# Weight conversion in the lead-in of a linear-attention and ELU-MLP kernel: first splits and lowerings earlier, most merges on GpSimd

## The chip, the cores and the metric

The kernel runs on one core of one Trainium2 chip. The metric is the device time in microseconds (us) of one execution; a time is the median of several runs. Engines are called by the names of the profile: PE (TensorE, the matrix engine; PEld is its weight load), DVE (VectorE), ACT (ScalarE), POOL (GpSimd) and SP (SyncE, which here only starts DMA transfers). Each engine works through its own queue in the order in which the program wrote the instructions; between engines, semaphores order the work.

## What is computed

The reference, cut to what matters:

```python
# attention: q, k, v, f_logit are (4, 8, 768, 48), float32
f = 1.0 / (1.0 + np.exp(-f_logit))
for t in range(S):
    state = f[:, :, t, :, None] * state + einsum('bhd,bhe->bhde', k[:, :, t], v[:, :, t])
    y[:, :, t] = einsum('bhd,bhde->bhe', q[:, :, t], state)
# mlp: x = y as (3072, 384); w_in (384, 2048), w_out (2048, 384), both float64
h = x @ w_in
g = np.where(h > 0.0, h, np.exp(np.minimum(h, 0.0)) - 1.0)
out = (g @ w_out).astype(np.float32)
```

The weights arrive in 64-bit floating point. The kernel turns them into 32-bit floating point itself, on the chip, while the first tokens are already being worked on. That conversion is what the change is about.

## The kernel before

Tokens are worked on in 12 units of 256. The attention of a unit writes `xt`; the MLP of the unit then multiplies it with `w_in` (an "up" product into the PSUM tile `psH`), applies the ELU and multiplies with `w_out` (a "down" product into `psM`). The weights are cut into 16 **items** of 128 x 768 numbers: eight blocks of `w_in` and eight of `w_out`, sorted by when the MLP first needs them. Items 0, 1, 2, 4, 6, 8 are the blocks 0 to 5 of `w_in`; items 3, 5, 7, 9, 10, 11 are the blocks 0 to 5 of `w_out`; items 12 to 15 are the last two of each.

Every item passes through four stages: `fetch` (DMA of the raw 64-bit words into one of AHEAD = 7 slots of `area`), `split` (two DVE instructions on the high halves), `lower` (one ACT instruction, which brings the top bits of the low halves into place) and `merge` (one 32-bit integer addition, after which the slot is free and the fetch seven items later is started).

```python
def split(n):
    raw = raws[n]
    hi = raw.bitcast(I32)[:, 1::2]
    bits = held[n] = sb.tile([128, 2 * DM], I32, tag="bits", name=f"bits{n}")   # two buffers, in turn
    nc.vector.tensor_scalar(out=bits[:], in0=hi, scalar1=3, scalar2=0x3FFFFFF8,          # L559
                            op0=ALU.logical_shift_left, op1=ALU.bitwise_and)
    nc.vector.tensor_scalar(out=hi, in0=hi, scalar1=-(2**30), scalar2=None, op0=ALU.bitwise_and)  # L563

def lower(n):
    nc.scalar.activation(raw.bitcast(U16)[:, 2::4], raw.bitcast(U32)[:, 0::2], AF.Copy, scale=2.0**-29)  # L569

def merge(n):
    ...
    nc.vector.tensor_tensor(out=to.bitcast(I32), in0=bits, in1=hi, op=ALU.add)            # L577
    fetch(n + AHEAD)
```

Other helpers that stand in the same stretch: `fall(u, p)` is a DVE reciprocal (L627), `scale(...)` a GpSimd multiplication of a 128x256 piece of q or k (L617), `move(u, which, queue)` two small DMAs from `f` to `f` (L634), started here from ACT's queue, `transposed` four PE transposes and an ACT copy (L665, L669), `first_outputs` the attention output of unit 0 (L804) with the ACT copies into `xt` (L814, L816), `watch` a tiny DVE check. The end of the lead-in, before the change:

```python
    step(0, NC - 1)
    split(0)
    ...                                   # GpSimd copies; fetches of items 2 to 6
    fall(1, 1)
    first_outputs(0)
    lower(0)
    merge(0)
    first_outputs(1)
    scale(1, ...k and q of pairs 0 to 2, on GpSimd...)
    split(1)
    transposed(1, 0, "a0")
    warm(1)                               # a matmul without use, for the PE clock
    transposed(1, 1, "a1")
    lower(1)
    watch(0)
    scale(1, ("q", 1, nc.gpsimd))
    fall(1, 2)
    scale(1, ("q", 2, nc.gpsimd))
    move(1, 1, nc.scalar)
    watch(1)
    at_step(1, lambda: scale(1, ("q", NKT, nc.gpsimd)))
    attention(1, (), A1)                  # attention of unit 1, its parts at the steps A1
    for n in range(1, NFT):
        t = max(needs[n][0] - 2, 0)       # two steps before the MLP needs item n
        at_step(t, lambda n=n: merge(n))
        if n > 1:
            later.setdefault(max(t - 2, 0), []).append(n)
```

After it comes a loop over steps T; two steps are one pair of an up product P = T // 2 and a down product P - 2:

```python
    for T in range(NU * NFT):
        P = T // 2
        if T % 2 == 0 and P and order[P - 1][0] < DIRECT:
            elu(P - 1)                    # DVE, L932: reads psH of P - 1 and so frees it
        for f in plan.pop(T, ()):         # what at_step put there
            f()
        if T % 2 == 0:
            up(P)                         # 12 matmuls, L923; psH has two buffers; then two ACT passes, L910, L911
        elif P >= LAG:
            down(P - LAG)                 # 8 matmuls, L955
        for n in later.pop(T, ()):
            split(n)
            lower(n)
```

The items 1 to 5 merge at the steps 0, 2, 3, 4, 5; items 6 to 15 at the steps 6, 7, 8, 9, 11, 13, 16, 20, 21 and 25. The attention of unit 1 has its parts `advance` (PE, L724), `step` (five DVE instructions, L682 and L687), `scores` and `mask` (PE L701, DVE L709), `outputs` (PE L739) and `carried` (PE L759) at the steps A1[1] to A1[5].

Of the kernel before, what the change touches and what calls it, by code (L numbers as in the profile page):

```python
# [9 lines left out]
I32 = mybir.dt.int32  # L10
# [3 lines left out]
ALU = mybir.AluOpType  # L14
# [342 lines left out]
def fast(ctx: ExitStack, tc: tile.TileContext, q, k, v, f_logit, w_in, w_out, out, flag, outer):  # L357
# [18 lines left out]
    nc = tc.nc  # L376
# [17 lines left out]
    LAG = 2  # L394
    AHEAD = 7
    WA = 1
    W0 = 3
    HOLD = 2
    A1 = (2, 4, 4, 5, 7, 9)
    D2 = (14, 16, 18, 20)  # L400
    A2 = (22, 24, 24, 26, 27, 28)
    D3 = (-7, -5, -3, -1)
# [67 lines left out]
    for y in first_y:  # L470
# [7 lines left out]
        out=causal[:], in_=causal[:], compare_op=ALU.is_ge, fill=0.0, base=0,  # L478
# [51 lines left out]
    def fetch(n):  # L530
        if n >= NFT:
            return
        j, out_ = parts[n]
        c = slice(j * 256, (j + 1) * 256)
        to = wo[:, 2 * j : 2 * j + 2] if out_ else wi[j][:]
        if wide:
            raws[n] = area[:, n % AHEAD]
            to = raws[n].rearrange("p (k f) -> p k f", k=to.shape[1])
        if out_:
            nc.sync.dma_start(out=to, in_=w_out[c, :].rearrange("(n p) f -> p n f", n=2))  # L540
            return
        nc.sync.dma_start(out=to[MAIN], in_=w_in[0 : NKT * 2 * D, c].rearrange("(k q) f -> q k f", k=NKT))
        rest = w_in[NKT * 2 * D :, c].rearrange("(r d k) f -> r d k f", r=2, d=PAD)
        for r in range(2):
            nc.sync.dma_start(out=to[GAP[r] : GAP[r] + PAD], in_=rest[r])
# [6 lines left out]
    def split(n):  # L552

        if not wide or n >= NFT:
            return
        raw = raws[n]
        hi = raw.bitcast(I32)[:, 1::2]
        bits = held[n] = sb.tile([128, 2 * DM], I32, tag="bits", name=f"bits{n}")
        nc.vector.tensor_scalar(  # L559
            out=bits[:], in0=hi, scalar1=3, scalar2=0x3FFFFFF8,  # L560
            op0=ALU.logical_shift_left, op1=ALU.bitwise_and,
        )
        nc.vector.tensor_scalar(out=hi, in0=hi, scalar1=-(2**30), scalar2=None, op0=ALU.bitwise_and)  # L563

    def lower(n):

        if wide and n < NFT:
# [4 lines that stand above are left out]
        if wide and n < NFT:  # L572
            hi = raws.pop(n).bitcast(I32)[:, 1::2]
            j, out_ = parts[n]
            to = wo[:, 2 * j : 2 * j + 2] if out_ else wi[j][:]
            bits, hi = (x.rearrange("p (k f) -> p k f", k=to.shape[1]) for x in (held.pop(n)[:], hi))
            nc.vector.tensor_tensor(out=to.bitcast(I32), in0=bits, in1=hi, op=ALU.add)  # L577
        fetch(n + AHEAD)


# [32 lines left out]
    def scale(u, *todo):  # L613

        t = qkf[u % NB]
        for n, p, e in todo:
            e.tensor_tensor(out=t[n][:, p], in0=t[n][:, p], in1=t["f"][:, p, "kq".index(n)], op=ALU.mult)  # L617
# [6 lines left out]
    def fall(u, p):  # L624

        f = qkf[u % NB]["f"]
        nc.vector.reciprocal(f[:, p, 1], f[:, p, 0])  # L627

    def move(u, which, queue):

        f = qkf[u % NB]["f"]
        for r in range(2):
            to = PAD + D * r
            queue.dma_start(out=f[to : to + D, NKT, which], in_=f[GAP[r] : GAP[r] + PAD, 0:NKT, which])  # L634
# [38 lines left out]
    def step(u, c):  # L673

        if u % UPB == UPB - 1 and c == NC - 1:
            return
        new = pus[u][c % 2][:, c // 2]
        box = boxes[(u * NC + c) % len(boxes)]
        s = box[:].rearrange("n (p d) -> n p d", d=64)[:, 0:HP, PAD:]
        if u % UPB or c:  # L680
            old = sts[u, c][:].rearrange("n (p d) -> n p d", d=64)[:, 0:HP, PAD:]
            nc.vector.tensor_tensor(out=s, in0=new, in1=old, op=ALU.add)  # L682
        else:
            nc.scalar.copy(s, new)
        if c == NC - 1:
            end = qkf[u % NB]["f"][:, :, 1, U - 1 :].broadcast_to([128, HP, D])
            nc.vector.tensor_tensor(out=s, in0=s, in1=end, op=ALU.mult)  # L687
        sts[(u, c + 1) if c < NC - 1 else (u + 1, 0)] = box
# [18 lines left out]
    def mask(u, pc):  # L707
        for r in range(2):
            nc.vector.tensor_tensor(  # L709
                out=ats[u][:, r].rearrange("k w p i -> k (w p) i"), in0=pc[r][:].rearrange("k w p i -> k (w p) i"),  # L710
                in1=twice[:].unsqueeze(1).broadcast_to([128, NW * HP, C]), op=ALU.mult,
            )
# [62 lines left out]
    def first_outputs(part):  # L775


        q_, at = qkf[0]["q"], ats[0]
        for gap in range(2):
            for w in range(NW):  # L780
                for p in range(NKT):
                    for r in range(2):
                        h = 2 * p + r
                        for b in range(2):
                            c = 2 * w + b
                            if part and c == 0:
                                continue
                            pair = NKT if gap else p
                            if gap:
                                cols = slice((1 - r) * PAD, (3 - r) * PAD)  # L790
                                lhs = (
                                    padded_s[FULL[r], c - 1, p, cols] if part
                                    else padded_v[FULL[b], w, r * NKT + p, cols]
                                )
                            elif part:
                                lhs = sts[0, c][FULL[r], 64 * p + r * PAD : 64 * (p + 1)]
                            else:
                                lhs = vs[0][FULL[b], w, PAD + h * D : PAD + (h + 1) * D] if r else even_v[FULL[b], w, p]
                            rhs = (
                                q_[FULL[r], pair, c * C : (c + 1) * C] if part else at[FULL[b], r, w, pair]  # L800
                            )
                            g = 64 * (r ^ b)
                            to = slice(g + 32 * r, g + 32 * r + 32) if gap else slice(g, g + (D if r else 64))
                            nc.tensor.matmul(  # L804
                                first_y[b][to, w, p], lhsT=lhs, rhs=rhs,
                                start=(part == gap == w == p == 0), stop=(part == 1), skip_group_check=True,
                            )
        if part == 0:
            for b in range(2):
                nc.scalar.copy(between[:, :, 0:NKT], first_y[b][:, :, :, 0])  # L810
            return
        x = xts[0] = sb.tile([128, HP + 1, U], FP32, tag="xt", name="xt0", bufs=3)
        to = x[:, 0:NKT].rearrange("n p (w b i) -> n b w p i", b=2, i=C)
        nc.scalar.copy(to[:, 0], first_y[0][:])  # L814
        for r in range(2):
            nc.scalar.copy(to[FULL[r], 1], first_y[1][FULL[1 - r]])  # L816

    plan, later = {}, {}

    def at_step(step, *todo):  # L820
        plan.setdefault(step, []).extend(todo)
# [218 lines left out]
    for n in range(1, HOLD):  # L1040
        fetch(n)
    warm(W0, "m3")
    for p in range(NKT):
# [7 lines left out]
    scale(0, ("q", 0, nc.gpsimd))  # L1051
    warm(WA, "m3")
    gates(1, bias=0)
# [28 lines left out]
    scores(0, None, (NKT,), pc)  # L1082
    warm(1)
    fall(1, 0)
    for c in range(NC - 1):
        step(0, c)
    mask(0, pc)
    step(0, NC - 1)
    split(0)
    for c in range(NC - 1):  # L1090
        nc.gpsimd.tensor_copy(
            padded_s[:, c, :, PAD : 2 * PAD],
# [4 lines left out]
        nc.gpsimd.memset(area[:, HOLD:].bitcast(I32)[:, :, 0:1], 0)  # L1097
    for n in range(HOLD, AHEAD):
        fetch(n)
    fall(1, 1)  # L1100
    first_outputs(0)
    lower(0)
    merge(0)
    first_outputs(1)
    scale(1, ("k", 0, nc.gpsimd), ("q", 0, nc.gpsimd), ("k", 1, nc.gpsimd), ("k", 2, nc.gpsimd))
    scale(1, ("k", NKT, nc.gpsimd))
    split(1)
    transposed(1, 0, "a0")
    warm(1)
    transposed(1, 1, "a1")  # L1110
    lower(1)
    watch(0)
    scale(1, ("q", 1, nc.gpsimd))
    fall(1, 2)
    scale(1, ("q", 2, nc.gpsimd))
    move(1, 1, nc.scalar)
    watch(1)
    at_step(1, lambda: scale(1, ("q", NKT, nc.gpsimd)))
    attention(1, (), A1)
    for n in range(1, NFT):  # L1120
        t = max(needs[n][0] - 2, 0)
        at_step(t, lambda n=n: merge(n))
        if n > 1:
            later.setdefault(max(t - 2, 0), []).append(n)
    at_step(4, lambda: load(2))
    at_step(12, lambda: gates(2))
    attention(2, D2, A2)
# [6 lines left out]
    for u in range(3, NU):  # L1134
        t = (u - 1) * NFT
# [4 lines left out]
    for n in range(NR):  # L1140
        t = 3 * NFT + (NU - 4) * NFT * n // NR + RR
# [73 lines left out]
```

## Time and profile before

| what | value |
|---|---|
| time | 569.17 us, median of 3 runs (569.11 to 569.18) |
| span of the profiled execution | 567.4 us |
| busy: PE, DVE, ACT, POOL | 550.2, 395.2, 229.3, 266.3 us |
| first up product starts | 29.25 us |
| L559, L563 (a split) on DVE | 0.56 us each in the median, 16 of each |
| L569 (a lowering) on ACT | 1.93 us in the median, 16 times |
| L577 (a merge) on DVE | 0.96 us in the median, 16 times |
| additions and multiplications on POOL | 128x128: 0.455 us (L942), 128x256: 0.72 us undisturbed (L617) |

How to read it: the span is the profiled execution from its first to its last instruction, a little less than the device time. Busy times are sums over the whole span and hide that the first 45 us are quite unlike the rest; so the queries by stretch of time matter more here than the totals. In a group line, the part after the first bar is the busy time in us and the mean in ns, the part after the second bar the engine's idle time before these instructions, with what ended it. In a timeline line, the columns are start, duration, engine, line and operation; square brackets give the idle time before it and what ended that.

### The profile page before, as it was taken

How to read it: one execution, taken by the hardware profiler on the slowest of the kernel's cores; microseconds unless marked ns; L12 is line 12 of the kernel's file. 1: busy time of each engine (PE TensorE's matmuls, PEld its weight loads, DVE VectorE, ACT ScalarE, POOL GpSimd, SP SyncE). 2: the span in 40 equal slices, each digit the busy share in tenths (PEclk: the TensorE clock that was granted, in tenths of full speed). 3: DMA queues.
4: the chain of work that ended last, by engine and by line, in shares of the span. 5: the costliest groups of instructions: out<-in, count | busy, mean ns of one | idle time of the engine just before them, and what ended most of it. 6: DMA issues, size and time to landing. Idle time of an engine off the chain costs nothing.

```text
span 567.4 us, 15202 instructions
## 1 busy us (share of the span) xinstructions
PE 550.2 (97%) x6226; PEld 501.8 (88%) x6226; DVE 395.2 (70%) x765; ACT 229.3 (40%) x417; POOL 266.3 (47%) x530
## 2 busy tenths in 40 slices
PE   6879999999999999999999999999999999999996
PEld 3457777778999999999999999999999999999995
DVE  8798485835976795885785885786786876745543
ACT  3297737334343443434333343343333343333331
POOL 6510027642374474465366357257257348325332
PEclk9998999999999999999999999999999999999999
DMA  8989780060025125215216216216206203201001
GB/s 207 259 215 297 174 223 14 2 161 29 2 50 140 58 60 143 73 45 152 79 36 155 85 37 154 84 38 154 84 20 172 84 9 72 85 2 36 29 2 35
DMA packets 37902, 53.27 MB, mean 94 GB/s; under 512 B 3680, under 2 KB 27648, under 8 KB 37824
## 3 DMA queue, kind: packets, MB, share of 16 engines
q1 hardware_dynamic: 37024, 51.62, 34.6%
q8 instruction: 51, 0.84, 0.6%
q10 hardware_dynamic: 800, 0.59, 0.5%
q14 instruction: 27, 0.22, 0.1%
HBM read 44.04 MB, written 4.72 MB: 86 GB/s over the span
## 4 chain that ended last, share of the span: by engine, by line
PE 92%; DVE 3%; DMA 2%; issue 1%; ACT 1%; POOL 1%; SPq 0%; DVEq 0%; ACTq 0%; POOLq 0%
PE psH L878 35%; PE psM L977 33%; PE psM L955 8%; PE psH L923 6%; PE psS L701 2%; PE psY L739 2%; PE psY L759 2%; PE psU_a L724 2%; PE psT L665 2%; DMA f<-f 1%; DVE f L627 1%; DMA f<-in_f_logit_dram 1%; ACT area L569 1%; DVE bits L559 0%; PE psY L804 0%
## 5 line engine op out<-in xcount | busy, mean ns | idle before, releaser
L878 PE MATMUL psH<-xt,wi 128*128 128x128 f32 (+1 forms) x960 | 177.1, 293 | 0.0
L942 POOL TENSOR_TENSOR sums<-gg 128x128 f32<-128x128 f32 x160 | 69.5, 455 | 210.8 <-DVE gg L932 202.5
L878 PEld LDWEIGHTS psH<-xt,wi 128*128 128x128 f32 x960 | 135.9, 192 | 0.8
L910 ACT ACTIVATE gg<-hh 128x512 f32<-128x512 f32 x80 | 50.5, 631 | 205.9 <-DVE hh L900 140.5
L878 PE MATMUL psH<-xt,area 128*128 128x128 f32 x640 | 110.5, 275 | 0.0
L878 PEld LDWEIGHTS psH<-xt,area 128*128 128x128 f32 x640 | 96.9, 192 | 4.1
L887 DVE TENSOR_TENSOR hh<-psH,u 128x256 f32<-128x256 f32 x80 | 33.8, 423 | 88.7 <-ACT u L885 88.7
L977 PE MATMUL psM<-area,sums 128*128 128x192 f32 x480 | 91.2, 326 | 0.0
L977 PEld LDWEIGHTS psM<-area,sums 128*128 128x128 f32 x480 | 80.1, 190 | 0.2 <-POOL sums L942 0.2
L977 PE MATMUL psM<-wo,gg 128*128 128x192 f32 x320 | 68.1, 335 | 0.0
L617 POOL TENSOR_TENSOR k<-k,f 128x256 f32<-128x256 f32 x48 | 39.4, 822 | 57.1 <-DMA area<-in_moe_w_in_dram 35.0
L627 DVE RECIPROCAL f<-f 128x256 f32<-128x256 f32 x36 | 62.8, 1747 | 1.3
L911 ACT ACTIVATE gg<-gg 128x512 f32<-128x512 f32 x96 | 60.6, 631 | 3.0
L932 DVE SCALAR_TENSOR_TENSOR gg<-gg,hh 128x512 f32<-128x512 f32 x80 | 55.7, 696 | 1.8 <-ACT gg L911 1.8
L977 PEld LDWEIGHTS psM<-wo,gg 128*128 128x128 f32 x320 | 50.2, 190 | 1.9
L900 DVE TENSOR_TENSOR hh<-psH,u43h 128x256 f32<-128x256 f32 (+1 forms) x160 | 49.8, 353 | 2.7
L923 PE MATMUL psH<-xt,wi 128*128 128x256 f32 x192 | 44.5, 381 | 1.4 <-DVE wi L577 1.2
L942 POOL TENSOR_TENSOR sums<-gg,sums 128x128 f32<-128x128 f32 x80 | 42.8, 535 | 6.3
L955 PE MATMUL psM<-wo,gg 128*128 128x384 f32 x128 | 45.4, 498 | 0.0
L885 ACT COPY u<-psH 128x128 f32<-128x128 f32 x80 | 21.0, 263 | 59.3 <-PE psH L878 59.3
L923 PEld LDWEIGHTS psH<-xt,wi 128*128 128x128 f32 x192 | 35.9, 190 | 8.6 <-issue 1.6
L900 DVE TENSOR_TENSOR u43h<-psH,hh 128x256 f32<-128x256 f32 x80 | 33.9, 423 | 13.4 <-PE psH L878 13.0
(97 smaller groups left out, 721.9 us busy)
## 6 DMA issues: line engine op xcount, KB each, us to landing
area<-in_moe_w_out_dram SPq DMA_DIRECT2D x8, 768.0 KB, 8.9
again<-in_moe_w_in_dram SPq DMA_DIRECT2D x16, 384.0 KB, 4.1
again<-in_moe_w_out_dram SPq DMA_DIRECT2D x16, 384.0 KB, 3.5
k<-in_k_dram SPq DMA_DIRECT2D x12, 384.0 KB, 4.8
q<-in_q_dram SPq DMA_DIRECT2D x12, 384.0 KB, 5.5
v<-in_v_dram SPq DMA_DIRECT2D x12, 384.0 KB, 5.9
area<-in_moe_w_in_dram SPq DMA_DIRECT2D x8, 576.0 KB, 7.2
out_dram<-o SPq DMA_DIRECT2D x38, 96.0 KB, 1.7
```

Source lines behind the costliest of these rows:

```text
L617: e.tensor_tensor(out=t[n][:, p], in0=t[n][:, p], in1=t["f"][:, p, "kq".index(n)], op=ALU.mult)
L627: nc.vector.reciprocal(f[:, p, 1], f[:, p, 0])
L878: nc.tensor.matmul(to, lhsT=lhs, rhs=rhs, start=(n == 0), stop=True, skip_group_check=True)
L887: add = lambda to, x, y: nc.vector.tensor_tensor(out=to, in0=x, in1=y, op=ALU.add)
L900: add = lambda to, x, y: nc.vector.tensor_tensor(out=to, in0=x, in1=y, op=ALU.add)
L910: nc.scalar.activation(g[:], h, AF.Relu, scale=-1.0)
L911: nc.scalar.activation(g[:], g[:], AF.Exp, scale=-1.0)
L923: nc.tensor.matmul(ph[:, i], lhsT=wi[j][:, kt, i * 128 : (i + 1) * 128], rhs=xts[m][:, kt, :], start=(kt == 0), stop=(kt == NKT - 1),)
L932: nc.vector.scalar_tensor_tensor(out=g[:], in0=g[:], scalar=-1.0, in1=phs.pop(P), op0=ALU.add, op1=ALU.max)
L942: nc.gpsimd.tensor_tensor(out=s[:, i], in0=x, in1=y, op=op)
L955: nc.tensor.matmul(pm[t][:], lhsT=g[:, i, t * 128 : (t + 1) * 128], rhs=wo[:, 2 * j + i, :], start=(j == 0 and i == 0), stop=(j == NP - 1 ...
L977: nc.tensor.matmul(pm[bank][:, half * DH : (half + 1) * DH], lhsT=x, rhs=y, start=first, stop=(j == NP - 1), skip_group_check=True,)
```

## The change

It reorders the conversion of the first items and moves most merges to another engine:

- `split(0)` and `lower(0)` stand before the mask of unit 0, `split(1)` and `lower(1)` where those of item 0 were, `merge(0)` right after the fetches.
- Both reciprocals that were left, `fall(1, 1)` and `fall(1, 2)`, follow one another, and `move(1, 1)` stands before the transposes.
- The split and lowering of items 2 and 3 come in step 0, ahead of the first up product, instead of after steps 0 and 1.
- Merges of item 2 and later run on GpSimd (M0 = 2); items 0 and 1 stay on DVE.
- The attention parts of unit 1 called `step`, `scores` and `outputs` come at the steps 5, 7, 8 instead of 4, 5, 7.

It is meant to have the weights ready sooner and to take work off the vector engine in the stretch in which that engine is fullest.

```diff
+    M0 = 2
-    A1 = (2, 4, 4, 5, 7, 9)
+    A1 = (2, 4, 5, 7, 8, 9)
@@ merge
-            nc.vector.tensor_tensor(out=to.bitcast(I32), in0=bits, in1=hi, op=ALU.add)
+            e = nc.gpsimd if n >= M0 else nc.vector
+            e.tensor_tensor(out=to.bitcast(I32), in0=bits, in1=hi, op=ALU.add)
@@ lead-in
     fall(1, 0)
+    split(0)
     for c in range(NC - 1):
         step(0, c)
+    lower(0)
     mask(0, pc)
     step(0, NC - 1)
-    split(0)
+    split(1)
 ...
     for n in range(HOLD, AHEAD):
         fetch(n)
+    merge(0)
     fall(1, 1)
+    fall(1, 2)
     first_outputs(0)
-    lower(0)
-    merge(0)
+    lower(1)
     first_outputs(1)
     scale(1, ("k", 0, nc.gpsimd), ("q", 0, nc.gpsimd), ("k", 1, nc.gpsimd), ("k", 2, nc.gpsimd))
     scale(1, ("k", NKT, nc.gpsimd))
-    split(1)
+    move(1, 1, nc.scalar)
     transposed(1, 0, "a0")
     warm(1)
     transposed(1, 1, "a1")
-    lower(1)
     watch(0)
-    scale(1, ("q", 1, nc.gpsimd))
-    fall(1, 2)
-    scale(1, ("q", 2, nc.gpsimd))
-    move(1, 1, nc.scalar)
+    scale(1, ("q", 1, nc.gpsimd), ("q", 2, nc.gpsimd))
     watch(1)
 ...
         if n > 1:
-            later.setdefault(max(t - 2, 0), []).append(n)
+            if t > 3:
+                later.setdefault(t - 2, []).append(n)
+            else:
+                at_step(0, lambda n=n: (split(n), lower(n)))
```

## Prediction

> **What bounds the kernel.** I first asked for the busy times by stretch.
>
> ```profile
> 29.10:45.00 15.90, 11.65 (x168) 9.47 (x166) 14.37 (x25) 13.62 (x13) 2.05 (x2) 0.96 0.87 219
> 45.00:62.00 17.00, 17.00 (x179) 11.95 (x179) 12.56 (x19) 12.15 (x14) 0.00 (x0) 0.94 1.06 284
> 62.00:125.00 63.00, 63.00 (x488) 46.55 (x487) 39.28 (x51) 31.16 (x41) 29.83 (x53) 1.00 0.42 106
> 125.00:280.00 155.00, 155.00 (x1861) 148.28 (x1860) 111.97 (x230) 59.76 (x122) 75.36 (x147) 1.00 0.28 77
> ```
>
> The columns are length, then PE, PEld, DVE, ACT and POOL busy, granted clock, DMA share, GB/s. From 45 us PE has no idle time at all; only the 5.4 us after its last product, at the very end, are without it. So a merge taken off DVE is worth nothing by itself, and the change can only pay before 45 us: by PE's waits there, and by a clock below 1. In that stretch DVE is 14.37/15.90 = 90% and ACT 86% busy, while POOL has 2.05 us of work. Next, the waits of PE and the chain of waits:
>
> ```profile
> PE psS L701 <- issue: 2.6, 1, 2.6
> ...
> PE psH L923 <- DVE wi L577: 1.2, 1, 1.2
> ...
> PE psS L701 <- DVE state L682: 0.2, 1, 0.2
> PE psH L923 <- PE psU_a L724: 0.2, 1, 0.2
> ```
>
> ```profile
> 34.27 1.96 ACT area L569
> ...
> 36.25 0.97 DVE wi L577
> 37.24 0.98 DVE bits L559
> ...
> 38.72 0.96 DVE wo L577
> 39.70 0.57 DVE bits L559
> ...
> 40.78 0.68 DVE gg L932
> ```
>
> In the first the numbers are us in total, times, longest; in the second start, length, engine and tile. The first up product starts at 29.25, the second waits 1.25 us for the merge of item 1 (on DVE from 31.98), and the scores of unit 1 wait 2.6 + 0.2 us: they need the state steps, which stand in DVE's queue behind the splits and merges of items 2 to 5. With the 0.2 us after `advance`, PE's waits after 29.25 sum to **4.25 us**. The last wait also costs clock: by one-us stretches it falls to 0.82 from 43 to 44, is 0.50 from 44 to 47 and 0.97 in the next, together 3.4 us at half speed. There the eight matmuls of the first down product take 3.81 us on the chain, later ones 2.58: **1.2 us** more. The ceiling is 4.25 + 1.2 = 5.5 us, 1.0% of 569.
>
> **What the Trainium skill says.** Three pages bear on it. "GPSIMD Engine Reference", section 4.1 (Engine selection), says an addition with all operands of one 32-bit integer type is exact there, so a merge is one plain instruction; section 3.1 puts two-input work at about 2.6 cycles an element, 2.2 ns at 1.2 GHz. The trace agrees: 128x128 takes 0.455 us and 128x256 0.72 undisturbed, (0.72 - 0.455)/128 = 2.07 ns an element and 0.19 us fixed. "SBUF — State Buffer", section "Who interferes with whom", says DVE and GpSimd share a port pair, held exclusively by whichever starts first, where the DVE instruction is in a 2-port mode or has two SBUF inputs. This case shows it:
>
> ```profile
> 36.25 0.96 DVE L577 CUSTOM_DVE_ANT_0 wi<-area,bits 128x1536 uint16<-128x1536 uint16 x1 [0.41 <-ACT area L569]
> 36.46 1.33 POOL L617 TENSOR_TENSOR q<-q,f 128x256 f32<-128x256 f32 x1 [4.17 <-DMA f<-f]
> ...
> 37.24 0.97 DVE L559 TENSOR_SCALAR bits<-area 128x768 int32<-128x768 int32 x1
> ```
>
> The multiplication that takes 0.72 lasts 1.33 behind a merge (until 37.79), and the split behind that 0.97 instead of 0.56, ending 0.42 after POOL is free. "TensorE: Matmul & The Clock Gate", Part 1, has PE's clock halved after an idle window of some 3.4 us; the 3.4 us at half speed after the wait of 2.6 agree.
>
> **The change part by part.**
>
> *Merge on GpSimd.* 0.19 + 768 x 2.07 ns = **1.78 us** (estimate; no 32-bit integer addition on POOL is in the trace), 0.8 more than DVE's 0.96 to 0.99. DVE loses 14 x 0.97 = 13.6 us, POOL gains 14 x 1.78 = 25 us. Up to 62 us POOL is empty, and later it is under half busy: room enough in sum. But `bits` has two buffers, so the split of item n waits for the merge of n - 2, and splits now contend with merges.
>
> *Item 0 earlier.* The merge at 27.73 ends 28.69, but the first up product waits for the ACT copies into `xt` (28.07 + 0.96 = 29.03). The lowering of item 1 takes the same place on ACT, 25.76 to 27.70. Gain: **0**; 29.25 stays.
>
> *Item 1 earlier.* Its fetch is started 14.90 to 16.45 and takes 7.2 to 8.0, so it lands about 24. Split 24.3 to 25.3, merge 0 to 26.2, two reciprocals of 1.75 to 29.7, merge 1 then 29.7 to 30.7, or 31.5 if a POOL scaling holds the port. The first up product ends at 31.8 (29.25 + 2.6): the 1.25 us wait goes.
>
> *Items 2 and 3 before the first up product.* This costs. ACT now has `move` at 29.7 (1.1 us of issuing), the two `kn` copies to 31.9, then two lowerings ahead of the ELU passes: after the split of item 2 (31.3 to 32.4), from 32.5 to 36.2. The ELU of product 0 follows at 36.2 instead of 32.83, and its end on DVE, which frees the `psH` buffer for the third up product, at 38.2 instead of 35.84. The third up product starts at about **38.2** (37.35 before), with PE idle since 35.4.
>
> *Steps and scores later.* Down product 0 and up product 3 come before the scores and fill most of the 2.6 us in which PE now waits. Needed are the merge of item 3 (done about 39, in time) and that of item 4.
>
> I laid the queues out with these durations, once for before and twice for after. For before, the layout has the up products at 33.4 and 37.5 and the scores at 43.4 (measured 33.25, 37.35, 43.29); all three go to the end of `carried`, with PE's work the same.
>
> *Layout A, no collisions.* DVE reaches its splits 0.7 us sooner, the third up product starts at 37.6, down 0 and up 3 follow without a gap, then scores, down 1. PE waits: 2.1 before up 2, 1.2 before `outputs` (the mask is late on DVE), 0.4 before `carried`; 3.8 against 5.4 in the layout of before. **-1.6 us**.
>
> *Layout B, port held exclusively, merge 1.78.* Merge 4 ends at 43.8, so up 3 waits 0.4 after down 0; split 6, waiting for merge 4 and then locked out by merge 5, ends at 46.5, and the state steps behind it give scores at 48.3 (wait 1.9); the mask behind splits 7 and 8 costs 1.5, and `carried` 0.8 behind a lowering. 2.8 + 0.4 + 1.9 + 1.5 + 0.8 = 7.4 against 5.4: **+1.9 us**.
>
> In both, the gaps are cut into pieces with products between them, so I take the half-speed stretch to go: **-1.2 us**. Sum: A -2.8, 566.4; B +0.7, 569.9. The port conflicts are real, but the layout makes each collision as bad as it can be, and with a merge of 1.2 us B comes to -1.1 before the clock. I choose a little below the middle: **567.9 us**.
>
> **Rivals.**
> - *GpSimd becomes the bound.* If an integer addition with 8-byte steps took far longer than 1.78 us, say 4, fourteen would be 56 us in one queue, in a chain through the two `bits` buffers; PE would stall at many steps and the time would go to 580 and more. Against it: the skill calls the addition native, and the floating point slope fits.
> - *DMA becomes the wait.* The DMA share is about 1 from 6 to 34 and from 38 to 62 us. Item 2 lands at 29.0 at the latest (fetched from 21.25 to 24.2), item 3 at 31.1 (24.39 + 6.7); their splits come after. The queue of SP waits 7.3 us for the `f<-f` transfer of `move` before it starts item 6 (36.15); with `move` 1.8 us earlier this starts earlier too. A wait taken away, but one that PE never saw: 0 us.
> - *The gap grows and the clock falls anyway.* If PE idles from 35.4 to 38.2 or longer inside one clock window, the 1.2 us come back: 567.6 (A) to 571.1 (B).
> - *POOL is late in the steps 20 to 28*, where it mixes weights without pause (from 89.85 to 99.88 in the trace). Three merges there add 5.3 us, but the mixes are first read at 124.6 and POOL finishes them at 106.6: hidden.
>
> **Range and chances.** Nothing reaches 2% (11.4 us) by gain, as the ceiling is 5.5. Range 565.4 to 571.2: a little under A, and B with the clock lost. Faster by over 2%: 0.01. Slower by over 2%: 0.03, the first rival. Within: 0.96.
>
> **What would show it.** The merge of items 2 and later as a POOL instruction of about 1.8 us; first up product at 29.2 and second at 31.8 to 32.0; third at 37.5 to 38.3; scores between 45.4 and 48.3, after two further products; splits of 0.9 us and more where a POOL merge runs (B) or all near 0.56 (A); no stretch of 0.50 clock between 40 and 60 us; PE without waits from about 60 us. The prediction is wrong if the merge is much off 1.78, if the first up product moves, or if PE waits after 60 us.

## The result and the profile after

The changed kernel takes **573.89 us** in the median (573.47 to 575.6, four runs) against 569.14 (568.74 to 569.18) for the kernel before on the same chip: a ratio of 1.0091, 95% interval 1.0070 to 1.0112. It is about 4.75 us slower. 567.9 was predicted, with a range that ended at 571.2: the prediction was wrong.

First the busy times of the changed kernel by the same stretches (length; PE, PEld, DVE, ACT and POOL busy; granted clock; DMA share; GB/s).

```profile
29.10:45.00 15.90, 10.44 (x98) 8.54 (x99) 9.04 (x14) 8.12 (x9) 5.05 (x4) 0.79 0.87 217
45.00:62.00 17.00, 14.62 (x172) 10.39 (x170) 12.09 (x19) 12.13 (x11) 9.40 (x5) 0.99 1.08 288
62.00:125.00 63.00, 62.84 (x542) 46.45 (x543) 36.93 (x46) 33.29 (x47) 39.62 (x55) 1.00 0.33 85
125.00:280.00 155.00, 155.00 (x1805) 147.10 (x1806) 108.94 (x223) 58.64 (x120) 76.55 (x148) 1.00 0.31 85
```

DVE fell from 14.37 to 9.04 us in the first stretch, as intended, but ACT fell too, from 13.62 to 8.12, and PE from 11.65 to 10.44, with the clock at 0.79 instead of 0.96. Only GpSimd's busy time rose, by the merges. Three engines had become idle together, so something that all of them need came late. The second stretch, full before, now has 2.4 us of PE idle. From 62 us on PE is as full as it was. The waits of PE:

```profile
PE psH L925 <- POOL wi L579: 5.5, 1, 5.5
...
PE psY L741 <- DVE at L711: 1.5, 2, 1.2
...
PE psS L703 <- PE psH L925: 0.6, 1, 0.6
...
PE psY L761 <- ACT between L748: 0.3, 1, 0.3
```

One wait of 5.5 us, for a merge on GpSimd, stands where 1.2 and 2.6 stood before. The chain of waits and GpSimd's timeline say why the merge was late:

```profile
30.52 7.77 DMA f<-f
...
38.43 0.09 POOL q L619
...
39.14 1.79 POOL wi L579
40.94 1.79 POOL wo L579
...
47.69 2.20 DVE bits L560
```

```profile
29.91 0.74 POOL L619 TENSOR_TENSOR q<-q,f 128x256 f32<-128x256 f32 x1 [0.89 <-DVE fine L648]
38.42 0.72 POOL L619 TENSOR_TENSOR q<-q,f 128x256 f32<-128x256 f32 x1 [7.78 <-DMA f<-f]
39.10 1.83 POOL L579 TENSOR_TENSOR wi<-bits,area 128x768 int32<-128x768 int32 x1
40.89 1.84 POOL L579 TENSOR_TENSOR wo<-bits,area 128x768 int32<-128x768 int32 x1
```

The program puts the scaling of the last piece of q (step 1) ahead of the merge of item 2 (step 2), and GpSimd works in that order. The scaling needs the small `f<-f` transfer of `move`. GpSimd stood idle for 7.78 us in front of it, with the merge ready behind it from about 34.5, when its lowering ended. The third up product then waits until 40.99 and runs mostly at half clock:

```profile
40.99 4.97 PE L925 MATMUL psH<-xt,wi 128*128 128x256 f32 x12 [5.46 <-POOL wi L579]
```

Of the 5.46 us, the ELU of product 0, which frees the `psH` buffer, accounts for 2.6 (2.8 were predicted); its end on DVE is at 38.09. The other 2.9 us are the merge behind the transfer.

```profile
37.40 0.69 DVE L934 SCALAR_TENSOR_TENSOR gg<-gg,psH 128x512 f32<-128x512 f32 x1 [3.79 <-ACT gg L913]
```

The sum: PE's waits after the first up product are 5.46 + 0.56 + 1.5 + 0.3 = 7.8 us against 4.25, so +3.6. The half-speed stretch is 6.83 us long (from 38.47) against 3.41, but PE works in only 4.3 us of it and loses half of that, 2.15 us, nearly all on this product (4.97 - 2.83). Before, PE worked all through the stretch and lost 1.7 us, on the scores and the first down product. So the clock adds only 0.4. The outputs and `carried` of unit 1 keep PE for 1.48 and 1.34 us instead of 1.16 each, +0.5. The first up product is 0.25 earlier. Together **+4.3 us**; the last down product of the two profiles ends at 561.90 and 566.23, 4.3 apart.

### The profile page after: what moved, and what is told of

It is laid out like the page before. It is cut to its first block, busy times and chain, and to the rows that moved or that the text cites. A ratio compares the mean times of both kernels' runs of the same rounds, so it can differ in the third digit from the quotient of the medians.

```text
span 571.5 us, 15211 instructions
## 1 busy us (share of the span) xinstructions
PE 551.7 (97%) x6226; PEld 503.0 (88%) x6226; DVE 389.9 (68%) x751; ACT 229.0 (40%) x417; POOL 291.4 (51%) x544
## 4 chain that ended last, share of the span: by engine, by line
PE 89%; DMA 4%; DVE 3%; POOL 2%; issue 1%; SPq 0%; ACTq 0%; DVEq 0%; ACT 0%; POOLq 0%
PE psH L880 34%; PE psM L979 33%; PE psM L957 6%; PE psH L925 6%; DMA f<-f 2%; PE psY L761 2%; PE psY L741 2%; PE psS L703 2%; PE psU_a L726 2%; PE psT L667 2%; DMA area<-in_moe_w_in_dram 1%; DMA k<-in_k_dram 1%; DVE bits L560 1%; POOL wi L579 1%; DVE f L629 1%
## 5 line engine op out<-in xcount | busy, mean ns | idle before, releaser
L925 PE MATMUL psH<-xt,wi 128*128 128x256 f32 x192 | 46.6, 395 | 5.7 <-POOL wi L579 5.5
L944 POOL TENSOR_TENSOR sums<-gg,sums 128x128 f32<-128x128 f32 x80 | 42.7, 534 | 6.3
L957 PE MATMUL psM<-wo,gg 128*128 128x384 f32 x128 | 44.2, 488 | 0.0
```

The source lines that it names most:

```text
L925: nc.tensor.matmul(ph[:, i], lhsT=wi[j][:, kt, i * 128 : (i + 1) * 128], rhs=xts[m][:, kt, :], start=(kt == 0), stop=(kt == NKT - 1),)
L944: nc.gpsimd.tensor_tensor(out=s[:, i], in0=x, in1=y, op=op)
L957: nc.tensor.matmul(pm[t][:], lhsT=g[:, i, t * 128 : (t + 1) * 128], rhs=wo[:, 2 * j + i, :], start=(j == 0 and i == 0), stop=(j == NP - 1 ...
```

## The experiments

Theory 1: the loss comes from the order in GpSimd's queue, merge behind a scaling that waits for a transfer. Theory 2: it comes from the merges being on GpSimd at all, from 0.9 us more for each and from splits of DVE held up at the shared port. The kernel before ran on the same chip beside each; its medians were 569.0 to 569.5. The place of the clock's windows and the start of the first up product (28.5 to 31.3 us) shift from execution to execution, so single profiles of one kernel differ by one or two us before the stretch in question; below, medians and ratios decide the times, profiles the causes.

**e1, the scaling behind the merges.** The changed kernel with one line moved.

```diff
-    at_step(1, lambda: scale(1, ("q", NKT, nc.gpsimd)))
+    at_step(5, lambda: scale(1, ("q", NKT, nc.gpsimd)))
```

> The changed kernel with one multiplication moved in GpSimd's queue: the scaling of q of the last pair of unit 1 stands behind the merges of items 2 to 5 (step 5) instead of ahead of them (step 1). Theory 1 (merge 2 comes late only because it stands behind this scaling, which waits for the f-to-f transfer): merge 2 runs at about 34.6 to 36.4, the third up product starts at 38.1 instead of 40.99, bounded by the ELU of product 0, and the time falls by 2.9 us and perhaps 1 more for the clock, to 569.5 to 571. Theory 2 (longer merges on GpSimd and port collisions are the cost): the four long splits of 2.1 to 2.2 us stay and the time stays above 573.

Measured: 571.8 us (four runs), ratio 1.0044 (1.0027 to 1.0061). GpSimd's timeline and PE's waits from 28 to 75 us:

```profile
35.66 1.86 POOL L579 TENSOR_TENSOR wi<-bits,area 128x768 int32<-128x768 int32 x1 [3.99 <-ACT area L570]
```

```profile
PE psH L925 <- DVE gg L934: 2.7, 1, 2.7
PE psH L925 <- DMA xt<-xt: 1.5, 1, 1.5
PE psY L741 <- DVE at L711: 1.5, 2, 1.2
```

The merge now follows its own input, the lowering, and the wait of 5.5 us becomes the 2.7 us for the ELU that the prediction had named. Half of the loss is gone. A **new wait of 1.5 us** shows before up product 6, for the small transfer inside `xt` of unit 1. The changed kernel has no such wait.

**e2, all merges on DVE** (`M0 = 99`, the order as changed).

> The changed kernel with all merges on DVE again; the reordering stays. Theory 1: merge 2 follows the first ELU on DVE (about 38.1 to 39.1), the third up product starts at 39.1 instead of 40.99; with some of the clock back, 570 to 571.5. Theory 2 (merges on GpSimd are the cost): the long splits vanish and the time falls below that of the kernel before, under 569. Theory 3 (the two lowerings ahead of the ELU passes are the cost): the third up product still starts 1.7 us later than before, 570 to 571.5 as well.

Measured: 572.03 us (four runs), ratio 1.0052 (1.0034 to 1.0069). No split takes 2 us any more, and the largest wait is 3.2 us for a merge on DVE. The time isn't told apart from e1's: taking the merges back and moving one scaling are worth the same, and neither restores the time before.

**e3, only the engine changed.** The kernel before, with the merges from item 2 on GpSimd and nothing moved.

> The kernel before with nothing changed but the merges of items 2 to 15, which run on GpSimd. Theory 1: merge 2 stands behind the scaling that waits for the f-to-f transfer (lands at about 36.4 there), so it runs at 37.2 to 39.0 and the third up product starts at 39.0 instead of 37.35; 570.5 to 572. Theory 2: collisions of splits with merges of 1.84 us show as splits of about 2.2 us, and the time is near the changed kernel's, 573 to 575.

Measured: 570.65 us (13 runs), ratio 1.0033 (1.0019 to 1.0047).

```profile
37.63 0.72 POOL L619 TENSOR_TENSOR q<-q,f 128x256 f32<-128x256 f32 x1 [5.79 <-DMA f<-f]
38.32 1.83 POOL L579 TENSOR_TENSOR wi<-bits,area 128x768 int32<-128x768 int32 x1
```

The same trap without any of the moves: merge 2 is ready before and stands behind the scaling; PE waits 3.5 us for it. The splits of over 2 us are here too (2.19 and 2.20 before 50 us), so its time doesn't part the two theories.

**e4 and e5, item 6 fetched later.** In the kernel before, SP's queue started item 6 only after a long wait for that same transfer; this is its own list of waits:

```profile
SPq L542 <- DMA f<-f: 7.7, 2, 7.3
```

In the changed kernel `move` starts at 29.91 instead of 31.56, yet lands at 38.3 instead of 36.4: item 6 is now started at 28.04, ahead of it. The packets of the small transfer move 6.2 us after its start in the median, against 2.8 before. e4 starts items 6 and 7 after `move`, by a memset on GpSimd that the fetch waits for; e5 later still, after merge 1.

```diff
 # e5, in merge(n); e4 has the same two fetches after move(1, 1)
+        if n == 1 and wide:
+            nc.vector.memset(area[:, AHEAD - 1 :].bitcast(I32)[:, :, 0:1], 0)
+        for i in (AHEAD - 1, AHEAD) if n == 1 else ():
+            fetch(i)
-        fetch(n + AHEAD)
+        if n:
+            fetch(n + AHEAD)
 # lead-in
-    for n in range(HOLD, AHEAD):
+    for n in range(HOLD, AHEAD - 1):
```

> The changed kernel with the fetch of item 6 held back until just after the f-to-f transfer of unit 1 has been started (its slot is cleared later, on GpSimd), as it was by accident in the kernel before. Theory 1a (the transfer lands 7.8 us after its start because item 6 had been put into the DMA queues ahead of it): it lands after about 4.5 to 5.5 us, at 35 or so, merge 2 ends by 37.5, the third up product starts at 38.1 and the time is 569.5 to 571. Theory 1b (the transfer is slow for another reason): it still lands at about 38, and the time stays at 573 to 574.5.

> As the run before it with the late fetch of item 6, but held back further, until the merge of item 1 on DVE is done, so that both halves of the f-to-f transfer are started first. In that earlier run the first half's packets moved 3.4 us after its start and only the second half, started beside the fetch, was overtaken. Theory 1a (first come, first served in the DMA queues): both halves land within about 5 us, merge 2 ends by 37.6 to 38 and the third up product starts about 9.1 us after the first (ELU of product 0) instead of 12.0; 571 to 572. Theory 1b (slow for another reason): it still takes 7 us or more, and the time stays above 573.

Measured: 574.25 us (four runs; 1.0098, 1.0077 to 1.0120) and 573.54 (five runs; 1.0072, 1.0048 to 1.0095). In e4 about two fifths of the packets moved by 35.3, but nearly all others at 36.5 to 38.1, beside item 6, which had been started close behind. In e5 the median packet moved at 34.1, 3.7 us after the start, but the last at 36.4:

```profile
37.59 0.73 POOL L624 TENSOR_TENSOR q<-q,f 128x256 f32<-128x256 f32 x1 [6.45 <-DMA f<-f]
```

By the lists of DMA issues, the transfer landed 7.4 us after its start in e4 and 6.7 in e5 (median of its two halves), against 7.8 in the changed kernel, 4.4 in the kernel before and 5.9 in e3, which has the old order up to there. So the start of item 6 has a part in it, about one microsecond of the landing and more of the median packet. The late last packets, which e3 has too (until 36.8), stay unexplained. In e5 PE's wait for merge 2 was 3.3 us instead of 5.5, but waits of 1.3 us for a later merge and of 1.1 before the scores came up, and the time isn't told from the changed kernel's. The page "DMA: Bandwidth & Descriptors" of the Trainium skill, section "Queues, rings and completion order", says a DMA engine takes turns, packet by packet, between the queues that have work. These two runs don't show a small transfer let through by that: its last packet in e5 moved 6.0 us after its start, and the scaling behind it began after that.

**e6, e7 and e9, the moves taken back in part.** e6 is e1 with item 3 split and lowered after the ELU of product 0. e7 is e6 with four buffers `bits` instead of two. e9 is the order of e6 for item 3 with all merges on DVE (`M0 = 99`) and the scaling of q at step 1.

```diff
-            if t > 3:
-                later.setdefault(t - 2, []).append(n)
+            if t > 2:
+                later.setdefault(max(t - 3, 0) if t == 3 else t - 2, []).append(n)
```

> The changed kernel with the scaling of q behind the merges of items 2 to 5, and, new here, split and lowering of item 3 after the ELU passes of product 0 instead of ahead of them. Theory 3 (the two lowerings ahead of the ELU passes delay the third up product): the ELU of product 0 ends 1.6 us earlier and the third up product starts 7.6 us after the first instead of 9.25, now bounded by merge 2; PE then waits about 1 us there instead of 2.7 and the clock holds: 569 to 570.5. If lowering 3 does not matter: 571.5 to 572 as in the run with the scaling alone.

> The run with scaling and item 3 moved, and four buffers for the upper bits instead of two, so that a split no longer waits for the merge two items earlier and no longer starts at the very moment a merge hands the port to the next one. Theory 2 (port collisions at the hand-over cost PE time): the splits of 2.1 to 2.2 us go from four to at most one or two, scores start 1 to 2 us earlier, and the time falls by another 1 to 2 us, to 567.5 to 569. If the collisions lie beside PE's work: the same time as with two buffers, within 0.5 us.

> The changed kernel with all merges on DVE and split and lowering of item 3 after the ELU passes of product 0. Theory 3: the third up product starts about 8.3 us after the first (the ELU ends on DVE, then merge 2) instead of 9.65 with the lowering ahead; no long splits; PE waits of about 2 us in the stretch; 569 to 570.5, against 572.0 with the lowering ahead. If the time stays at 571.5 to 572, lowering 3 is not what held that version back.

Measured: 571.75 (7 runs; 1.0034, 1.0012 to 1.0055), 571.17 (20 runs; 1.0033, 1.0018 to 1.0049) and 571.38 us (12 runs; 1.0031, 1.0010 to 1.0052). The third up product starts 8.05 us after the first in e6, 1.2 us sooner than in e1 (9.25), and the time is no better. Twice the buffers change nothing, but e7 kept its long splits (three of about 2.1 us and two of 1.55 and 1.82 before 60 us), so it says little about what they cost. In all three a wait of 1.6 to 1.8 us for `xt` stands later. PE's waits from 26 to 75 us in e9:

```profile
PE psH L925 <- DVE wi L579: 1.9, 1, 1.9
PE psY L741 <- DVE at L711: 1.9, 2, 1.6
PE psH L925 <- DMA xt<-xt: 1.6, 1, 1.6
```

That pointed away from the engines and to the second transfer.

**g1 and h1, the clock by itself.** The changed kernel with matmuls without use in the gap of 5.5 us: nine, then four.

```diff
     attention(1, (), A1)
+    at_step(4, lambda: warm(9, "m3"))       # h1: warm(4, "m3")
```

> The changed kernel with nine useless matmuls of the kind of warm put at step 4, after advance, where PE stands still for 5.5 us. Theory 1 (the half-speed stretch of 6.8 us behind that gap is a cost of its own, about 2.1 us on the third up product, which took 4.97 us instead of 2.83): the clock stays full through 38 to 46 us, the third up product still starts at about 41 because the merge of item 2 is as late as ever, but takes about 2.8 us, and the time is about 571.8, 2 below the changed kernel. Rival (the half-speed stretch comes whatever PE does, or the useless matmuls push the third up product back): the product still takes over 4 us or starts later than 42, and the time stays at 573 to 574.5.

> The changed kernel with four useless matmuls after advance. In g1 nine took 8.0 us, 0.89 each, so four run from about 37.1 to 40.7 and end before the merge of item 2 does (41 to 41.5). Theory 1 (PE's idle time costs the clock): clock full from 38 to 46 us, third up product at about 41 and 2.8 us long instead of 4.97, time about 571.8, 2.1 below the changed kernel. Rival (the half-speed stretch comes anyway or moves elsewhere): 573.5 to 574.5.

Measured: 575.1 (five runs; 1.0091, 1.0059 to 1.0123) and 574.73 us (five runs; 1.0106, 1.0082 to 1.0130). Neither gained. PE's timeline of g1 and then of h1:

```profile
37.10 7.99 PE L1034 MATMUL psW<-ident 128*128 128x512 f32 x18
```

```profile
41.69 4.54 PE L925 MATMUL psH<-xt,wi 128*128 128x256 f32 x12 [2.31 <-POOL wi L579]
```

The dose of g1 was wrong: nine matmuls took 8.0 us, ended at 44.9, and the third up product, ready at about 41.6, waited for them. There was no half-speed stretch there and the product took 2.75 us. Counted from the start of the first up product, it began 2.2 us later than in the changed kernel, took 2.2 us less and ended at the same point, 16.9 us: what the clock gave, the useless matmuls took. In h1 the four ended at 39.4, and the 2.31 us of idle time that were left still cost the following 3.4 us at half speed. So an idle PE does bring the clock down, but a gain from filling the gap was not shown here.

**h2 and h3, the order of transfers.** h2 is the changed kernel, h3 is e1, both with the transfer inside `xt` of unit 1 started from SP, where the loads of unit 2 and the fetches of items 12 to 15 now come behind it.

```diff
-            (nc.sync if u > 1 else nc.scalar).dma_start(
+            nc.sync.dma_start(
 ...
-        fetch(n + AHEAD)
+        if n + AHEAD < 12:
+            fetch(n + AHEAD)
 ...
-    at_step(4, lambda: load(2))
+    at_step(4, lambda: load(2, "f"))
+    at_step(10, lambda: load(2, "kqv"))
+    for n in range(12, NFT):
+        at_step(n - 2, lambda n=n: fetch(n))
```

> The changed kernel with only the order of transfers changed as in g2: the one inside xt of unit 1 from SP, and unit 2's loads and the fetches of items 12 to 15 behind it. Theory 1 (the wait for xt is hidden while the wait for the merge of item 2 holds PE back): no gain, 573 to 574.5. Rival (the transfers posted early cost something by themselves): 572 or less.

> e1 (the scaling of the last q piece at step 5, behind merges 2 to 5 in GpSimd's queue; merges on GpSimd, everything else as changed) with the order of transfers of h2. Theory 1 (two waits in series: with the first gone the second shows, 1.5 us in e1): the wait for xt before up product 6 goes, time about 570.2, 1.5 below e1. Rival: e1's time stays, 571.5 to 572.

Measured: h2 574.95 us (five runs; 1.0089, 1.0068 to 1.0111), no gain at all; **h3 569.47 us** (13 runs; 0.9998, 0.9986 to 1.0011), the time of the kernel before. PE's waits from 28 to 75 us in h3:

```profile
PE psH L926 <- DVE gg L935: 2.7, 1, 2.7
PE psY L742 <- DVE at L712: 1.5, 2, 1.2
PE psS L704 <- issue: 1.4, 1, 1.4
```

No wait for `xt` is left. From the lists of DMA issues from 26 to 70 us, with the median from issue to landing in us at the end, first of e1 and then of h3:

```profile
xt<-xt ACTq DMA_DIRECT2D x2, 48.0 KB, 7.5
```

```profile
xt<-xt SPq DMA_DIRECT2D x2, 48.0 KB, 2.2
```

In the kernel before it takes 5.0 and in the changed one 3.0. It lands the sooner the less the DMA engines have to do just then: their busy share was 0.16 in the 2.2 us after its start in h3 (60.33), 0.35 in the 3 us after it in the changed kernel (64.7), 0.67 in 5 us in the kernel before (60.3) and 0.84 in 7.5 us in e1 (61.7). In the changed kernel the first wait has pushed its start 3 us back, behind most of the weights, and no wait for it shows. The same edit is worth nothing in h2 and 0.46% (2.6 us by the ratios) in h3: the second wait comes up only when the first no longer holds PE back, so it can't be seen, or gained, in the changed kernel. With both gone the whole loss is gone, though all merges from item 2 on are still on GpSimd. The edit does three things at once (the queue of the small transfer, the loads and the fetches that now come later); which of them matters was not tried. h3's profile also has no half-speed stretch from 10 us to the end of PE's work, e1's had one of 3.4 us; but what PE saves by it, it waits longer for the scores (1.44 us in h3, none in e1).

**g2, g3 and g4, what the moves are worth then.** g2 is e9 with the order of transfers of h2. g3 adds three matmuls without use ahead of the outputs. g4 is g3 with the merges on GpSimd again and the scaling at step 5.

```diff
+    at_step(8, lambda: warm(3, "m3"))       # g3, g4
     attention(1, (), A1)
```

> e9 (all merges on DVE, item 3 split and lowered after the ELU passes of product 0) with the transfer inside xt of unit 1 started from SP instead of ACT, and the loads of unit 2 and the fetches of items 12 to 15 put behind it. Theory 1 (with the f-to-f wait gone, what is left before up product 6 is a wait of 1.6 us for that transfer, which lands late because weights and loads were posted ahead of it): the wait before up product 6 goes below 0.3, the stretch from the first up product to the end of the third down product stays at about 32.5, and the time is about 569.7, 1.6 below e9. Rival (the transfer is late for another reason, or the fetches placed later are now themselves late): the wait stays at 1.5 or comes back at another product, and the time stays at 571 or more.

> g2 with three useless matmuls of the kind of warm at step 8, ahead of the outputs of unit 1, where PE waits 1.9 us for the mask and the clock then falls to half for 3.4 us. Theory 1 (the idle time costs the clock): the dip at 54 to 57 us goes, 1.7 us are gained, and the time is about 568, a little below the kernel before. Rival (the dip is set by the window of small matmuls around the scores and not by the idle time, or it comes elsewhere): a dip of 3.4 us is still there and the time is that of g2, about 569.7.

> g3 with the merges from item 2 on GpSimd again and the scaling of the last q piece at step 5, so that no merge stands behind the f-to-f transfer. Theory 2 (the longer merge and the lengthened splits behind it cost about 1 us by themselves): splits of about 2.1 us come back, waits of PE for POOL or for the mask grow, and the time is 0.8 to 1.5 above g3, about 569. Rival (only the queue behind the f-to-f transfer cost anything): within 0.4 of g3.

Measured: g2 568.06 us (20 runs; 0.9978, 0.9964 to 0.9992), g3 **567.76** (18 runs; 0.9973, 0.9962 to 0.9985), g4 569.4 (13 runs; 1.0002, 0.9983 to 1.0020). g2 and g3 are faster than the kernel before by 0.2 to 0.3%, and than the changed one by over 1%. The three matmuls of g3 add nothing that can be measured (1.7 us had been expected); in g2's own profile the half-speed stretch lies at 40.27 and not where they stand. GpSimd's timeline and PE's waits from 26 to 75 us in g3:

```profile
40.17 0.80 POOL L620 TENSOR_TENSOR q<-q,f 128x256 f32<-128x256 f32 x1 [9.06 <-DMA f<-f]
```

```profile
PE psH L926 <- DVE wi L579: 1.8, 1, 1.8
PE psH L926 <- ACT xt L819: 0.7, 1, 0.7
```

The first line is the plainest evidence for theory 1. The same scaling waits 9.06 us for the same transfer, 1.75 us later than in the changed kernel, and PE has no wait for it, because no merge stands behind it. g4 is 0.29% above g3, 1.6 us (the two intervals just touch): theory 2's share, for the merges, lengthened splits and the place of the scaling together. In g4 a split of 1.83 us delays the steps, and the scores wait for them:

```profile
PE psS L704 <- issue: 1.9, 1, 1.9
```

**The profiles side by side.** In each, PE's work from the start of the first up product to the end of the last down product can be taken apart into idle time, time lost at half speed (half of what PE worked there) and the rest; all in us. The useless matmuls of g3 and g4 count as work.

| run | ratio | first up product starts | from there to PE's last | idle | lost at half speed |
|---|---|---|---|---|---|
| before | 1 | 29.25 | 532.65 | 4.2 | 1.7 |
| changed | 1.0091 | 29.00 | 537.23 | 8.0 | 2.2 |
| e1 | 1.0044 | 30.02 | 534.89 | 6.2 | 1.5 |
| e2 | 1.0052 | 31.25 | 532.95 | 4.5 | 1.6 |
| e3 | 1.0033 | 28.67 | 534.83 | 6.5 | 1.7 |
| h3 | 0.9998 | 28.49 | 533.37 | 6.1 | 0.0 |
| g3 | 0.9973 | 29.47 | 531.00 | 1.9 | 0.0 |
| g4 | 1.0002 | 29.15 | 533.30 | 3.5 | 0.0 |

From e1 to h3 this stretch shrinks by 1.52 us, which is the wait for `xt`. e2 differs from the kernel before by only 0.3 us in it; its time is long because the first up product starts late. In the 15 profiles with the changed lead-in that product starts between 28.49 and 31.30, at 29.85 in the mean; in the two with the old one at 28.67 and 29.25. Whether the new lead-in costs time ahead of that product is not shown.

## Why the prediction was wrong, step by step

**The step that failed is the transfer.** The rival "DMA becomes the wait" closed with "A wait taken away, but one that PE never saw: 0 us", and the layouts had the merge of item 3 "done about 39, in time"; it ended at 42.7. The line that would have shown it stood in the prediction itself: the multiplication at 36.46 was quoted for its length, while its bracket, 4.17 us of waiting for `f<-f`, was passed over. In the kernel before that wait was harmless, since GpSimd had nothing else to do. The change put fourteen merges into the same queue, the first of them right behind it. With the landing unchanged, 36.46 + 0.72 + 1.83 = 39.0 was already the earliest start of the third up product, 0.8 us after the 38.2 predicted. The landing came 2 us later still, which makes 41. e1, h3 and g3 show the first part; why the transfer lands later is settled only in part (e4, e5).

**The clock.** "I take the half-speed stretch to go: -1.2 us" failed: it became twice as long and cost 0.4 us more. (The 1.2 counted the first down product alone; with the scores the stretch of the kernel before cost 1.7.) The gap was to be cut into pieces; it became one of 5.5 us instead. The rival "the gap grows and the clock falls anyway" had this right, for a smaller gap.

**Layouts A and B.** The port collisions of B were real. In the changed kernel five instructions of the splits were drawn out to 2.09 to 2.21 us, such as this one on DVE:

```profile
40.97 2.18 DVE L560 TENSOR_SCALAR bits<-area 128x768 int32<-128x768 int32 x1 [2.88 <-POOL wi L579]
```

By their sum B's waits (7.4 us) were close to those measured (7.8), but for another reason: 5.5 instead of 2.8 before the third up product, 0.56 instead of 1.9 before the scores, 1.5 before the outputs as predicted, 0.3 instead of 0.8 before `carried`. Going below the middle of A and B towards A was the wrong choice, but B with the clock lost, 571.1, was still 2.8 us short. Part of this lies in the layout itself: for the kernel before it had 5.4 us of waits where 4.25 had been measured. Counted from the measured value, B with the clock lost is 572.3.

**What held.** The merge was estimated at 1.78 us and took:

```profile
L579 POOL TENSOR_TENSOR wo<-bits,area x8: 1835/1844/1945, 40.9 to 106.5; 128x768 int32<-128x768 int32 x8
```

(shortest, median and longest in ns). The first up product stayed, 29.00 for 29.25. The second came directly behind it, without its 1.25 us. Taking off DVE's load was worth nothing (g4, with the merges on GpSimd, is the slower of the pair), and the seven merges on GpSimd that begin after 62 us cost nothing. GpSimd did not become the bound. The scores came at 51.7, outside 45.4 to 48.3, as everything after the third up product was late.

**What stays open.** e1 to h3 gave 2.6 us by the ratios, with an interval of about 1.2 us either way, where the wait for `xt` was 1.5. The profiles give 1.5 from the first up product on; whether the rest is more than scatter ahead of that product is not shown. Why `f<-f` lands so much later in the changed kernel is explained only in part, by the start of item 6. For the kernel before, it was not tried whether `xt` lands in time there because SP was held up for 7 us and posted fewer transfers.

## What to carry to other kernels

Before work is moved to an idle engine, read what that engine is idle for: a queue works in order, and an instruction that waits for a transfer, harmless while nothing stands behind it, holds back everything that is put there. Put the work with a late input last. Taking one wait away can bring up the next, at another transfer, so judge such an edit only after the next has been removed as well, as h2 and h3 do.

## What the runs showed of the hardware

**Where a gap lies among the clock's windows decides.** The changes of the clock in each profile lie on a grid of 3.413 us whose place differs from run to run. The Trainium skill's "TensorE: Matmul & The Clock Gate", Part 1, has this window, free-running, and the traces agree. What they add is how much of it must be idle. I cut the 17 profiles by their own grids, from 26 to 70 us, and summed PE's idle time in each window. All 12 windows with 1.86 us or more of it were followed by one at half speed, and none with less than 1.49 us. Of the 14 from 1.49 to 1.78 us three were; what parts them wasn't found. So the 2.73 us gap of h3, cut by the grid into 1.51 and 1.22, cost no clock, while the 2.31 us of h1, inside one window, did.

**A small transfer beside the weights is slow.** The transfer inside `xt` (two of 48 KB) took 2.2 us to land with the DMA engines 16% busy (h3) and 7.5 with them 84% busy (e1). `f<-f` took 4.4 us in the kernel before, 5.9 in e3 with the same order, 7.8 in the changed kernel and 8.0 and 8.7 in g2 and g3. An earlier start did not make it land earlier.
